# Two attention steps and two MLPs on one core: a prologue in another order, weights narrowed 512 wide at fixed steps, and the first MLP's product taken one step behind its halves

## The chip, the cores and the metric

The kernel runs on one core of one Trainium2 chip. A core has a matmul engine (PE, with its weight loads listed apart as PEld), a vector engine (DVE), an activation engine (ACT), a general engine (POOL), and SP, which here only issues DMAs. Each engine works through its own list of instructions in order, and waits on semaphores for what other engines make. The metric is the device time of one execution in microseconds (us). The kernel before takes 996.47 us, the median of three runs from 996.24 to 996.62.

## The reference

`x` is 12480 x 128, `inducing` 32 x 128; both MLPs have w_in 128 x 2048 and w_out 2048 x 128.

```python
def mab(q, kv):
    s = scale * (q @ kv.transpose(0, 2, 1))
    s = s - s.max(-1, keepdims=True)
    a = np.exp(s)
    a /= a.sum(-1, keepdims=True) + 1e-09
    return a @ kv
h = mab(I, x)                 # 32 x 128: the inducing rows attend to all of x
y = mab(x, h)                 # 12480 x 128: every row of x attends to h
y = (g * np.cos(g)) @ w_out   # first MLP, g = y @ w_in
y = (g * sigmoid(g)) @ w_out  # second MLP, g = y @ w_in
```

The weights arrive as 64-bit floats, which the chip does not compute with; the kernel reads them as pairs of 32-bit words and builds 32-bit floats itself.

## The kernel before

**Prologue.** `h` needs a pass over the whole of `x` before any row of the second attention can start. `x` is loaded in eight heads (L70) of 8, 16, 16, 16, 16, 16, 6 and 4 tiles of 128 rows. For each head, PE transposes its tiles (L389), ACT and DVE copy them out of PSUM (`untile`, L400 to L405), PE forms the scores (L420), DVE their maximum (`mx`, L430), ACT the exponentials (L480), DVE turns them (`et`, L503), and PE sums over `x` (L535). After the last head, `hT4` holds `h` transposed (L641), PE multiplies it into the first MLP's w_in (`project`, L657), and ACT and DVE make `hw` of it (L666, L669): the attention's second product and the first MLP's w_in are one matrix.

**Blocks and steps.** The 12480 rows are cut into 26 blocks of at most 512 rows. For each block a softmax over 32 weights per row gives `ahi` and `at`, the upper and lower half of the weights; four copies of them stacked on the partitions (`stk`, two buffers, used in turn) are the moving operand of the first MLP. The softmax is done by chunks of four blocks, the first chunk being two blocks. Blocks 0 and 1 get their stack from PE (L712) and an ACT copy (L720); all later ones from DMAs on SP's queue (`spread`, L296).

A block is eight units of 256 hidden columns, and step `s` of the main loop takes unit `s` through the first MLP and unit `s - 11` through the second: `mlp1_in(s)` (L768, PE) reads `stk` and `hw`; `mlp1_act(s)` (L797, ACT cosine; L801, DVE product; L808, DVE upper half `hi`); `mlp1_rest(s)` (L819, DVE lower half `lo`); `mlp1_out(s - D1)` with D1 = 2 (PE); `mlp2_in(s - 11)` (L877, PE), `mlp2_act` (L892 and L900 on ACT, L901 on POOL) and `mlp2_out(s - 13)` (PE). The hidden tile `h1` has two PSUM buffers, so `mlp1_in(s)` waits until DVE is done with unit `s - 2`; `h2` has one. A product into an output is either three passes over halves (`down`, L829) or, while the halves of the weights are not made yet, two full 32-bit matmuls (`down_whole`, L839): for the first two blocks of the first MLP (16 units), and the first block of the second (8 units).

**Narrowing.** Each of the four weight matrices is narrowed in 8 pieces of 256 columns: a DMA fetches 64-bit words into `raw`, ACT makes `body` and `tail` (L126, L127), DVE `sign` and the joined word (L132, L137), POOL adds the tail (L147). w_out and the second w_in are then split into halves by ACT (L161) and POOL (L162). 15 pieces are narrowed in the prologue, among the heads' work, and 17 in the main loop, from lists that the functions `words`, `signs`, `join` and `splits` take from. Every engine's order is the order in which the code is written.

Of the kernel before, what the change touches and what calls it, by code (L numbers as in the profile page):

```python
# [21 lines left out]
def tile_induced_attention_then_two_mlps(  # L22
# [47 lines left out]
    heads = [(90, 8), (0, 16), (16, 16), (32, 16), (48, 16), (64, 16), (80, 6), (86, 4)]  # L70
# [26 lines left out]
    EARLY = 15  # L97
    PC, RAW = 2 * P, 4
    cv = ctx.enter_context(tc.tile_pool(name="cv", bufs=2, reuse_waits="tile"))
# [3 lines left out]
        "out1": lambda j: w_out1.rearrange("(f p) d -> p f d", p=P)[:, 2 * j : 2 * j + 2, :],  # L103
        "out2": lambda j: w_out2.rearrange("(f p) d -> p f d", p=P)[:, 2 * j : 2 * j + 2, :],
    }
    raws = {}
    order = [(name, j) for name in ("in1", "out1", "in2", "out2") for j in range(NJ)]
    pieces = order[:EARLY]

    def fetch():  # L110
        if not pieces:
            return
        name, j = pieces.pop(0)
        raw = cv.tile([P, PC], I64, tag="raw", name="raw", bufs=RAW)
        dst = raw if name[0] == "i" else raw.rearrange("p (f d) -> p f d", f=2)
        nc.sync.dma_start(out=dst, in_=views[name](j))
        raws[name, j] = raw
# [3 lines left out]
    def narrow_words(name, j):  # L121
        words = raws.pop((name, j)).bitcast(I32).rearrange("p (n w) -> p n w", w=2)
        low, high = words[:, :, 0], words[:, :, 1]
        body = cv.tile([P, PC], F32, tag="body", name="body")
        tail = cv.tile([P, PC], I32, tag="tail", name="tail")
# [50 lines left out]

    def join(n=1):
        for _ in range(n):
            if not wait_join:
                signs()  # L180
            if wait_join:
                name, j = wait_join.pop(0)
                if name == "in1":
                    narrow_join(name, j, win[:, j * PC : (j + 1) * PC])
                elif name[0] == "o":
                    v = whole_of[name][:, 2 * j : 2 * j + 2, :].rearrange("p f d -> p (f d)")
                    narrow_join(name, j, v)
# [34 lines left out]

    def weigh_take(st):
        nt = st["span"][1]
        s2 = st["pool"].tile([P, nt, M], F32, tag="s2", name="s2t")
        nc.vector.transpose(s2.rearrange("p t m -> p (t m)"), st["ps"])  # L226
        st["e"] = s2

    def weigh_centre(st, eng):
        nt, s2 = st["span"][1], st["e"]  # L230
        m2 = st["pool"].tile([P, nt, 1], F32, tag="m2", name="m2")
        nc.vector.tensor_reduce(out=m2, in_=s2, axis=AX.X, op=ALU.max)
        eng.tensor_tensor(s2, s2, m2.to_broadcast([P, nt, M]), ALU.subtract)

    def weigh_exp(st):
        nc.scalar.activation(st["e"], st["e"], AF.Exp, scale=scale)  # L236

    def weigh_norm(st, eng, between=()):
        nt, e = st["span"][1], st["e"]
        sm = st["pool"].tile([P, nt, 1], F32, tag="sm", name="sm")  # L240
        between = iter(between)
        nc.vector.tensor_reduce(out=sm, in_=e, axis=AX.X, op=ALU.add)
        next(between, int)()
        nc.vector.tensor_scalar_add(sm, sm, 1e-9)
        next(between, int)()
        nc.vector.reciprocal(sm, sm)
        next(between, int)()
        eng.tensor_tensor(e, e, sm.to_broadcast([P, nt, M]), ALU.mult)

    def weigh_turn(st):  # L250
        at = st["pool"].tile([P, st["span"][1] * Q], F32, tag="at", name="at")
        nc.vector.transpose(at, st["e"].rearrange("p t m -> p (t m)"))
        st["at"] = at

    def weigh_split(st, eng):
        at = st["at"]
        n = st["span"][1] * Q
        hi = st["pool"].tile([P, n], F32R, tag="ahi", name="ahi")
        nc.scalar.copy(hi, at)
        eng.tensor_tensor(at, at, hi.bitcast(F32), ALU.subtract)  # L260
        st["hi"], st["lo"] = hi.bitcast(F32), at
# [12 lines left out]
    NU = NB * NJ  # L274
    stacks = {}
# [13 lines left out]
    def spread(b, st):  # L289
        t0 = chunks[blocks[b][0]][0]  # L290
        stack = stk[:, b % 2, :]
        for g, t, m, at, n in places(b):
            a = (t - t0) * Q
            for r in range(G):
                src = st["hi"] if r < 2 else st["lo"]
# [6 lines left out]
    with ExitStack() as pro:  # L302
# [31 lines left out]
        AHEAD = 2  # L334
        PRE = (2, 2)
        for k in range(AHEAD):
            load(k)
            for _ in range(PRE[k]):
# [711 lines left out]
```

## Time and profile before

| | us |
|---|---|
| median of 3 runs | 996.47 |
| profiled execution | 998.4 |
| its span (first to last instruction) | 996.6 |
| mean granted TensorE clock | 0.997 of full speed |

The page gives, for each engine, how long it was busy; rows of the trace give single instructions: start, duration, engine, line, output <- input, shape, and in brackets how long the engine stood idle before it and what it then waited for.

### The profile page before, as it was taken

The numbers are of one execution on the slowest core, as the hardware profiler recorded it, in microseconds if no ns is written. First come the engines' busy times: TensorE is split into PE (matmuls) and PEld (weight loads), VectorE is DVE, ScalarE is ACT, GpSimd is POOL, SyncE is SP. The second block draws the span as 40 slices with busy tenths as digits, with TensorE's granted clock in tenths as the row PEclk, the third lists the DMA queues.
The fourth block names the chain that finished last, engine by engine and source line by source line (L and its number), as shares of the span: only waits on it lengthen the run. The fifth ranks groups of instructions, "written<-read, shape, count | busy, mean of one in ns | idle before, by whom it ended". The sixth has DMA issues, their size and how long they took to land.

```text
span 996.6 us, 12618 instructions
## 1 busy us (share of the span) xinstructions
PE 970.7 (97%) x4687; PEld 775.5 (78%) x4687; DVE 782.6 (79%) x843; ACT 708.7 (71%) x810; POOL 512.7 (51%) x293
## 2 busy tenths in 40 slices
PE   9987999999999999999999999999999999999996
PEld 6644577788887788887788887788887788889996
DVE  4875588888888888888888888888888888767871
ACT  5778666777676777676777676777676777677774
POOL 2334355564555564555564555565555554565554
PEclk9999999999999999999999999999999999999999
DMA  8432010110110100110100100100100100000001
GB/s 284 134 108 62 22 21 1 22 25 9 22 19 3 22 13 9 22 19 4 22 12 11 22 16 5 22 12 11 22 16 6 21 11 8 18 18 16 9 8 17
DMA packets 65744, 27.98 MB, mean 28 GB/s; under 512 B 54312, under 2 KB 59656, under 8 KB 65672
## 3 DMA queue, kind: packets, MB, share of 16 engines
q1 hardware_dynamic: 65016, 26.98, 11.2%
q8 instruction: 39, 0.64, 0.3%
q14 instruction: 33, 0.27, 0.1%
q10 hardware_dynamic: 656, 0.09, 0.1%
HBM read 14.79 MB, written 6.39 MB: 21 GB/s over the span
## 4 chain that ended last, share of the span: by engine, by line
PE 88%; ACT 3%; issue 2%; DVE 2%; POOL 1%; POOLq 0%; DVEq 0%; ACTq 0%
PE acc L829 49%; PE h L877 27%; PE h L768 8%; PE acc L839 3%; ACT c L797 1%; ACT L892 1%; ACT s L892 1%; PE s L215 1%; DVE c L801 0%; DVE s2t L226 0%; ACT s2t L236 0%; PE hwps L657 0%; ACT L236 0%; DVE sign L137 0%; DVE sign L132 0%
## 5 line engine op out<-in xcount | busy, mean ns | idle before, releaser
L901 POOL TENSOR_TENSOR lo<-s,hi 128x1024 fp32r<-128x1024 f32 (+2 forms) x197 | 447.9, 2274 | 389.1 <-ACT hi L900 343.0
L829 PE MATMUL acc<-hi,wo 128*128 128x512 f32 (+2 forms) x1568 | 403.0, 379 | 0.0
L797 ACT ACTIVATE c<-h,half_pi 128x1024 f32<-128x1024 f32 (+2 forms) x208 | 221.1, 1063 | 158.0 <-PE h L768 157.9
L829 PEld LDWEIGHTS acc<-hi,wo 128*128 128x128 f32 x1568 | 285.5, 188 | 55.0 <-issue 1.4
L801 DVE TENSOR_TENSOR h<-h,c 128x1024 f32<-128x1024 f32 (+2 forms) x192 | 222.7, 1160 | 132.6 <-ACT c L797 132.3
L877 PE MATMUL h<-yhi,wi 128*128 128x512 f32 (+2 forms) x832 | 248.0, 380 | 6.7 <-ACT s L892 5.9
L892 ACT ACTIVATE s<-h 128x1024 f32<-128x1024 f32 (+2 forms) x208 | 202.3, 973 | 66.1 <-PE h L877 64.4
L829 PE MATMUL acc<-lo,wo 128*128 128x512 f32 (+2 forms) x784 | 232.8, 378 | 0.1
L808 DVE CAST hi<-h 128x1024 fp32r<-128x1024 f32 (+2 forms) x192 | 221.2, 1152 | 6.6
L819 DVE TENSOR_TENSOR lo<-h,hi 128x1024 fp32r<-128x1024 f32 (+2 forms) x192 | 220.2, 1147 | 5.7
L900 ACT CAST hi<-s 128x1024 fp32r<-128x1024 f32 (+2 forms) x197 | 196.6, 998 | 6.3
L877 PEld LDWEIGHTS h<-yhi,wi 128*128 128x128 f32 x832 | 151.3, 188 | 41.0 <-ACT s L892 10.4
L829 PEld LDWEIGHTS acc<-lo,wo 128*128 128x128 f32 x784 | 144.2, 188 | 29.2 <-POOL lo L906 0.4
L877 PE MATMUL h<-ylo,wi 128*128 128x512 f32 (+2 forms) x416 | 156.9, 377 | 0.0
L768 PE MATMUL h<-stk,hw 128*128 128x512 f32 (+2 forms) x416 | 128.8, 391 | 7.5 <-DVE c L801 6.8
L768 PEld LDWEIGHTS h<-stk,hw 128*128 128x128 f32 x416 | 76.1, 189 | 35.3 <-DVE c L801 12.2
L877 PEld LDWEIGHTS h<-ylo,wi 128*128 128x128 f32 x416 | 78.1, 188 | 14.5
L801 DVE TENSOR_TENSOR c<-h,c 128x1024 f32<-128x1024 f32 x16 | 19.5, 1222 | 19.8 <-ACT c L797 17.6
L839 PE MATMUL acc<-c,wf 128*128 128x512 f32 x64 | 31.2, 612 | 0.9 <-DVE ylo L863 0.9
L862 ACT CAST yhi<-acc 128x512 fp32r<-128x512 f32 (+2 forms) x26 | 14.6, 561 | 15.8 <-PE acc L829 12.3
L127 ACT ACTIVATE tail<-raw 128x256 int32<-128x256 uint32 x32 | 13.9, 435 | 13.6 <-POOL held L147 8.1
L863 DVE TENSOR_TENSOR ylo<-acc,yhi 128x512 fp32r<-128x512 f32 (+2 forms) x26 | 16.9, 651 | 8.4 <-ACT yhi L862 8.3
(138 smaller groups left out, 371.5 us busy)
## 6 DMA issues: line engine op xcount, KB each, us to landing
x_sb<-in_x_dram SPq DMA_DIRECT2D x10, 512.0 KB, 6.0
out_dram<-o SPq DMA_DIRECT2D x80, 64.0 KB, 2.0
raw<-in_moe_w_in_dram SPq DMA_DIRECT2D x16, 256.0 KB, 3.5
raw<-in_moe_w_out_dram SPq DMA_DIRECT2D x16, 256.0 KB, 2.8
stk<-ahi SPq DMA_DIRECT2D x40, 64.0 KB, 2.0
stk<-at SPq DMA_DIRECT2D x40, 64.0 KB, 2.0
x_sb<-in_x_dram SPq DMA_DIRECT2D x3, 192.0 KB, 4.5
out_dram<-o SPq DMA_DIRECT2D x34, 16.0 KB, 1.5
```

What stands on the lines that cost most here:

```text
L768: nc.tensor.matmul(ps[:, a, 0:n], lhsT=hw[f // 4][:, f % 4 * P : (f % 4 + 1) * P], rhs=stacks[b][:, 0:n], start=True, stop=True,)
L797: nc.scalar.activation(cs, h, AF.Sin, bias=half_pi, scale=1.0)
L801: nc.vector.tensor_tensor(cs if whole else h, h, cs, ALU.mult)
L808: nc.vector.tensor_copy(hi[:, :, 0:n], h)
L819: nc.vector.tensor_tensor(lo[:, :, 0:n], h, hi[:, :, 0:n].bitcast(F32), ALU.subtract)
L829: nc.tensor.matmul(acc[:, 0:n], lhsT=wt[:, 2 * j + a, :], rhs=gt[:, a, 0:n], start=(j == 0 and p == 0 and a == 0), stop=(j == NJ - 1 and p ...
L839: nc.tensor.matmul(acc[:, 0:n], lhsT=w[:, 2 * j + a, :], rhs=c[:, a, 0:n], start=(j == 0 and a == 0), stop=(j == NJ - 1 and a == 1),)
L863: nc.vector.tensor_tensor(lo[:, 0:n], y[:, 0:n], hi[:, 0:n].bitcast(F32), ALU.subtract)
L877: nc.tensor.matmul(ps[:, a, 0:n], lhsT=wt[:, fs], rhs=yt[:, 0:n], start=(p == 0), stop=(p == 2),)
L892: nc.scalar.activation(sv, hid2.pop(u)[:, :, 0:n], AF.Silu)
L900: nc.scalar.copy(hv, sv)
L901: nc.gpsimd.tensor_tensor(lv, sv, hv.bitcast(F32), ALU.subtract)
```

## The change

- **Prologue.** All of `x` is issued first, with three fetches of weights among its last heads; the heads are 8, 10, 16, 16, 16, 16, 11 and 5 tiles, and the ten tiles with the ragged end come second. Five pieces are narrowed there instead of fifteen, and they are 512 wide: one each beside heads 3 to 6, one after the last. DVE alone copies the last head's second half.
- **First blocks.** Before the main loop only block 0's softmax is finished, and only its stack comes from PE. Block 1's softmax is begun there (scores, centre, exponentials), normed at step 1, turned at 2, split at 3, and its stack is spread by DMA at step 4. Its weights lie in four groups of 128 columns, so the spread is 16 DMAs. The flag that picks the cosine's form is made after block 0's weights.
- **Main loop.** 11 pieces of 512 columns are narrowed at steps 0, 1, 2, 3, 5, 7, 9, 11, 12, 14 and 16 and split at fixed steps, with one buffer each of `body` and `sign`, two of `tail` and three of `raw`. Chunk 1's softmax takes steps 3 to 14 (its exponentials at 11 instead of 6), and block 2's stack is spread at step 15 instead of 13.
- **First MLP.** `mlp1_out` follows one step behind from unit 12 on, and full matmuls are used for 12 units instead of 16. `hi1` and `lo1` have two buffers instead of three.

```diff
-    heads = [(90, 8), (0, 16), (16, 16), (32, 16), (48, 16), (64, 16), (80, 6), (86, 4)]
+    heads = [(0, 8), (88, 10), (8, 16), (24, 16), (40, 16), (56, 16), (72, 11), (83, 5)]
...
-    EARLY = 15
-    PC, RAW = 2 * P, 4
-    cv = ctx.enter_context(tc.tile_pool(name="cv", bufs=2, reuse_waits="tile"))
+    EARLY = 5
+    PF = 4
+    PC, RAW = PF * P, 3
+    NP = NF // PF
+    raw = persist.tile([P, RAW, PC], I64, name="raw")
+    cv = ctx.enter_context(tc.tile_pool(name="cv", bufs=1, reuse_waits="tile"))
...
+    def narrow(name, j):
+
+        narrow_words(name, j)
+        yield
+        narrow_sign(name, j)
...
+            narrow_join(name, j, v)
...
+        fetch()
...
+    def begin(k):
+        step = narrow(*order[k])
+        next(step)
+        return lambda: next(step, None)
...
-        for k in range(AHEAD):
+        for k in range(NH):
             load(k)
-            for _ in range(PRE[k]):
+            if 3 <= k < 3 + RAW:
                 fetch()
...
+        beside = {3: 0, 4: 1, 5: 2, 6: 3}
         for i in range(end):
-            if i + AHEAD < NH:
-                load(i + AHEAD)
+            finish = None
...
             if i >= 1:
                 bias(i - 1)
                 exps(i - 1)
-                splits()
-                words()
+            if i in beside:
+                finish = begin(beside[i])
...
             if i >= 1:
                 turn(i - 1)
-            if 1 <= i < end - 1:
-                join()
+            if finish:
+                finish()
...
+        soft = [weigh_view(MT * b, MT, MT * b) for b in range(2)]
...
+        weigh_exp(soft[1])
         nc.scalar.activation(warm, ones, AF.Silu)
...
-    WHOLE1, WHOLE2 = 2, 1
+    WHOLE1, WHOLE2 = 12, 8
...
+    narrowing = dict(zip((0, 1, 2, 3, 5, 7, 9, 11, 12, 14, 16), order[EARLY:]))
+    splitting = dict(zip((4, 6, 8, 10), order[2 * NP : 3 * NP]))
+    splitting.update(zip((13, 15, 11, 12), order[NP : 2 * NP]))
+    splitting.update(zip((17, 18, 19, 20), order[3 * NP :]))
+
+    second = {1: "norm", 2: "turn", 3: "split"}
+    third = {3: "take", 5: "centre", 11: "exp", 12: "norm", 13: "turn", 14: "split"}
+    later = {0: "take", 2: "centre", 5: "exp", 7: "norm", 10: "turn", 11: "split"}
+
+    def d1(u):
+        return 2 if u < WHOLE1 else 1
...
         def fill(s):
-            for b in range(first_of[1], NB):
-                if s + (FILL0 if blocks[b][0] == 1 else FILL) == b * NJ:
-                    spread(b, ast)
+            for b in range(1, NB):
+                if s == (4 if b == 1 else b * NJ - (1 if b == 2 else FILL)):
+                    spread(b, chunk_soft[blocks[b][0]] if b > 1 else soft[1])
```

DVE in the loop over the heads, one turn from the scores' maximum to the next turn's copy: before,

```order
L430 TENSOR_REDUCE mx<-s_492 128x1
L503 STREAM_TRANSPOSE et<-e 128x512
L510 SCALAR_TENSOR_TENSOR zacc_167<-zacc_166,al,zk 128x1
L132 TENSOR_SCALAR sign<-raw 128x256
L137 SCALAR_TENSOR_TENSOR sign<-body,sign 128x256
L442 TENSOR_REDUCE rm<-misc 1x32
L402 COPY xT<-pt 128x2x256
```

and now, beside heads 3 to 6:

```order
L431 TENSOR_REDUCE mx<-s_414 128x1
L504 STREAM_TRANSPOSE et<-e 128x512
L511 SCALAR_TENSOR_TENSOR zacc_180<-zacc_179,al,zk 128x1
L143 TENSOR_SCALAR sign<-raw 128x512
L148 SCALAR_TENSOR_TENSOR sign<-body,sign 128x512
L443 TENSOR_REDUCE rm<-misc 1x32
L403 COPY xT<-pt 128x2x256
```

The two narrowing instructions stand at the same place and are twice as wide; the other pair of a turn, which stood behind `hacc`, is gone.

SP around the first stack that comes by DMA (`ahi` and `at` are the halves of the softmax's weights, `stk` the stack): before,

```order
L116 DMA raw<-in_moe_w_in_dram 128x256 x8
L116 DMA raw<-in_moe_w_out_dram 128x2x128 x8
L296 DMA stk<-ahi 32x512 x2
L296 DMA stk<-at 32x512 x2
```

where that is block 2's; and now, where block 1's comes first:

```order
L127 DMA raw<-in_moe_w_in_dram 128x512 x4
L297 DMA stk<-ahi 32x128 x2
L297 DMA stk<-at 32x128 x2
L297 DMA stk<-ahi 32x128 x2
L297 DMA stk<-at 32x128 x2
L297 DMA stk<-ahi 32x128 x2
L297 DMA stk<-at 32x128 x2
L297 DMA stk<-ahi 32x128 x2
L297 DMA stk<-at 32x128 x2
L127 DMA raw<-in_moe_w_out_dram 128x4x128 x4
L297 DMA stk<-ahi 32x512 x2
L297 DMA stk<-at 32x512 x2
```

Sixteen small DMAs are new, between the second w_in's last four fetches and the second w_out's.

POOL from step 2 on, in the changed kernel (line 158 is the narrowing's add, 173 the split's lower half, 261 the lower half `at` of a softmax's weights, 244 and 254 its centring and norming):

```order
L158 TENSOR_TENSOR wf_63<-sign,tail 128x512
L158 TENSOR_TENSOR tail<-sign,tail 128x512
L261 TENSOR_TENSOR at<-at,ahi 128x128
L173 TENSOR_TENSOR wi_1_768<-tail,wi_0_767 128x512
L158 TENSOR_TENSOR tail<-sign,tail 128x512
L244 TENSOR_TENSOR s_72<-s_72,m_73 128x512
L173 TENSOR_TENSOR wi_1_768<-tail,wi_0_767 128x512
```

Block 1's `at` stands behind the add of step 3's piece; before, block 1 had no `at` on POOL at all.

## Rows read from the trace of the kernel before

**Rows 1.** Stretches: us; PE, PEld, DVE, ACT, POOL busy; clock, DMA, GB/s.

```profile
54.09:94.67 40.58, 31.56 (x91) 15.72 (x91) 27.03 (x43) 32.00 (x55) 17.04 (x23) 0.96 0.28 83
...
140.00:945.00 805.00, 799.98 (x3612) 655.42 (x3611) 666.76 (x610) 581.47 (x582) 437.20 (x198) 1.00 0.08 15
```

**Rows 2.** PE's `mlp1_in`: start us, us, what, idle before. Units 0-1, 8, 9, 13.

```profile
54.09 1.20 PE L768 MATMUL h<-stk,hw 128*128 128x512 f32 x4 [0.67 <-ACT stk L720]
...
72.71 0.72 PE L768 MATMUL h<-stk,hw 128*128 128x512 f32 x2
79.16 1.22 PE L768 MATMUL h<-stk,hw 128*128 128x512 f32 x2 [4.00 <-DVE c L801]
...
94.67 1.03 PE L768 MATMUL h<-stk,hw 128*128 128x512 f32 x2
```

**Rows 3.** One turn of the loop over the heads, PE and DVE.

```profile
24.62 1.09 PE L389 MATMUL pt<-ident,x_sb 128*128 128x128 f32 x8
...
26.07 0.29 DVE L132 TENSOR_SCALAR sign<-raw 128x256 int32<-128x256 int32 x1
26.46 0.42 DVE L137 SCALAR_TENSOR_TENSOR sign<-body,sign 128x256 int32<-128x256 int32 x1
26.80 0.27 DVE L442 TENSOR_REDUCE rm<-misc 1x32 f32<-1x128 f32 x1
...
29.32 1.09 PE L389 MATMUL pt<-ident,x_sb 128*128 128x128 f32 x8
```

**Rows 4.** End of the prologue: `hT4`, ACT's copies of `hw` and `stk`.

```profile
45.22 0.28 DVE L641 COPY hT<-misc 128x128 f32<-128x128 f32 x1
...
50.10 2.03 ACT L666 CAST hw<-hwps 128x512 fp32r<-128x512 f32 x4
...
53.45 0.58 ACT L720 CAST stk<-st 128x512 fp32r<-128x512 f32 x1 [0.31 <-PE st L712]
```

**Rows 5.** Groups by form to 130 us: count, busy us, mean ns, idle before.

```profile
L797 ACT ACTIVATE c<-h,half_pi 128x1024 f32<-128x1024 f32 x20 | 22.2, 1112 | 3.9 <-PE h L768 3.9
L801 DVE TENSOR_TENSOR c<-h,c 128x1024 f32<-128x1024 f32 x16 | 19.5, 1222 | 19.8 <-ACT c L797 17.6 <-issue 2.1
...
L147 POOL TENSOR_TENSOR tail<-sign,tail 128x256 int32<-128x256 int32 x8 | 5.8, 724 | 11.6 <-DVE sign L137 8.0 <-ACT wi L161 2.5 <-ACT tail L127 1.1
...
L236 ACT ACT_TABLE_LOAD x1 | 1.3, 1283 | 0.0
...
L260 POOL TENSOR_TENSOR at<-at,ahi 128x512 f32<-128x512 f32 x1 | 1.3, 1280 | 0.0
L862 ACT CAST yhi<-acc 128x512 fp32r<-128x512 f32 x2 | 1.2, 588 | 3.2 <-PE acc L839 3.2
```

**Rows 6.** SP's issues: start us, us for all of them, count.

```profile
100.27 1.25 SPq L296 DMA_DIRECT2D stk<-ahi  x2
...
136.32 7.50 SPq L934 DMA_DIRECT2D out_dram<-o  x16
```

**Rows 7.** Page part 6: KB each, median us from issue to landing.

```profile
stk<-ahi SPq DMA_DIRECT2D x40, 64.0 KB, 2.0
...
out_dram<-o SPq DMA_DIRECT2D x34, 16.0 KB, 1.5
```

**Rows 8.** Granted clock (third from the right) after PE's pause from 75.16 us.

```profile
78.00:79.00 1.00, 0.00 (x0) 0.00 (x0) 1.00 (x1) 1.00 (x4) 0.00 (x0) 0.96 0.00 0
...
82.00:83.00 1.00, 1.00 (x4) 0.43 (x3) 0.93 (x4) 0.15 (x1) 0.72 (x1) 0.83 0.10 22
```

**Rows 9.** Chain of waits: one full product, and two products by halves.

```profile
93.51 1.72 PE acc L839 x4
...
138.33 2.78 PE acc L829 x12
```

**Rows 10.** A step in mid-run: DVE's last half, PE's next step.

```profile
516.63 1.22 DVE L819 TENSOR_TENSOR lo<-h,hi 128x1024 fp32r<-128x1024 f32 x1
516.90 0.62 PE L768 MATMUL h<-stk,hw 128*128 128x512 f32 x2
```

More of the change, by code (lines that the diff above doesn't have):

```diff
@@ L246, in weigh_norm @@
         nc.vector.reciprocal(sm, sm)
-        next(between, int)()
-        eng.tensor_tensor(e, e, sm.to_broadcast([P, nt, M]), ALU.mult)
+        eng.tensor_tensor(e, e, sm.to_broadcast(list(e.shape)), ALU.mult)
     def weigh_turn(st):
[L251 to L261, printed above, removed]
+        nc.vector.transpose(st["at"], flat(st["s2"]))
@@ L274, in tile_induced_attention_then_two_mlps @@
     NU = NB * NJ
+    chunk_soft = [weigh_view(*span) for span in chunks]
     stacks = {}
@@ new lines, in tile_induced_attention_then_two_mlps @@
+        top = ps_s.tile([P, W], F32, tag="s1", name="st")
+        for i, v in enumerate((hi0, lo0)):
+            for g, t, m, at, n in places(0):
+                nc.tensor.matmul(
+                    top[:, at : at + n],
+                    lhsT=pick[:, g, 2 - 2 * i : 6 - 2 * i, :].rearrange("p r m -> p (r m)"),
+                    rhs=v[:, t * Q : t * Q + n],
+                    start=(i == 0 and g == 0),
+                    stop=(i == 1 and g == G - 1),
+                )
+        nc.scalar.copy(stk[:, 0, :], top)
@@ new lines, in soften @@
+        def soften(st, what):
+            if what == "take":
+                ps = psh.tile([P, 2, 512], F32, tag="h2", name="s2")
+                weigh_scores(st, ps[:, 0, 0 : st["span"][1] * Q])
+                weigh_take(st)
+            elif what == "centre":
+                weigh_centre(st, nc.gpsimd)
+            elif what == "exp":
+                weigh_exp(st)
+            elif what == "norm":
+                weigh_norm(st, nc.gpsimd)
+            elif what == "turn":
+                weigh_turn(st)
+            elif what == "split":
+                weigh_split(st, nc.scalar.copy, nc.gpsimd)
@@ L973, in fill @@
+        def attend(s, early):
+            todo = [(soft[1], second.get(s)), (chunk_soft[1], third.get(s))]
+            for k in range(2, NK):
+                todo.append((chunk_soft[k], later.get(s + LEAD - first_of[k] * NJ)))
+            for st, what in todo:
+                if what and (what == "exp") == early:
+                    soften(st, what)
         def fill(s):
-            for b in range(first_of[1], NB):
-                if s + (FILL0 if blocks[b][0] == 1 else FILL) == b * NJ:
-                    spread(b, ast)
+            for b in range(1, NB):
+                if s == (4 if b == 1 else b * NJ - (1 if b == 2 else FILL)):
+                    spread(b, chunk_soft[blocks[b][0]] if b > 1 else soft[1])
```

291 lines of the change are left out of this document (108 added, 183 removed).

## Prediction, made before the changed kernel was run

> **What bounds the kernel now.** I read the busy times of each engine by stretches first. From 140 to 945 us PE is busy 799.98 of 805.00 us at a granted clock of 1.00 [rows 1]: whatever the change does there counts only if it adds or removes PE work, or makes PE wait. From 54.09 to 94.67, in the loop's first steps, PE is busy only 31.56 of 40.58, and no engine is busy all the time (ACT 32.00, DVE 27.03, POOL 17.04): a chain that passes from engine to engine sets the pace. Next I read PE's starts of `mlp1_in` one by one [rows 2]. Unit 0 starts at 54.09, unit 8 at 72.71, unit 9 after 4.00 us of waiting at 79.16, unit 13 at 94.67; from there on PE never waits long. So the kernel has three parts: a prologue of 54.09 us, a ragged stretch of 40.58 us, and a full PE. The change has to be priced in the first two, and by what it takes off PE's work in the third.
>
> **The prologue.** A turn of the loop over the heads takes 29.32 - 24.62 = 4.70 us [rows 3]. DVE's chain sets it, and `sign` and join stand in that chain, from 26.07 to 26.80, before `rm`: 0.73 us. The changed turn has the same two there, 512 wide. No row shows that form. A join of 256 is 0.42; doubling the columns adds some 0.27 (an ACT or DVE form of 512 is about 0.2 to 0.3 longer than one of 256), `sign` adds some 0.13: 0.4 us more a turn, bounds 0 and 0.73 (no change, twice as long). Turn by turn: the second head has six tiles less, about -2.0; the two following turns without narrowing -0.2 each; four turns with it +0.4 each; the last two heads have six tiles more, +1.8; narrowing that left the tail of the prologue -0.6. Sum +0.4, so `hT4` comes at about 45.7 instead of 45.22 [rows 4]. With the bounds it is between 42.5 and 47.
>
> From `hT4` to unit 0 it was 8.87 us. Now only block 0's softmax is on the way, at 128 columns instead of 256, and DVE has no narrowing there. But ACT is late next: its exponentials, the table load of 1.28, four copies into `hw` (2.03 for four) and one copy into `stk` (0.58) instead of two [rows 4, 5] end about 6.8 us after `hT4`. That is 2.05 less. The prologue's sum is -1.6, bounds -5 and +1.
>
> **Steps 0 to 12 without new waits.** Count t from unit 0. In steps 0 to 3 there is one buffer of `sign`: DVE's `sign` (start to join 0.52), join (0.70, and 0.14 until POOL starts), POOL's add, then the next `sign`. POOL's add of 256 takes 0.72 and its 512-wide subtraction 1.28 [rows 5]; I take 1.28 plus 0.04. That ring is 2.7 us a step, more than ACT's cosine and two narrowing instructions (2.1), and with a first `sign` at t = 3.3 and the softmax's small pieces the one of step 3 starts at 11.6. From step 4 on pieces come every second step and ACT has to copy the piece's upper half, made by POOL, before the next cosine: cosine 1.14, product 1.14 (1.11 and 1.22 busy), `sign` 0.52, join 0.84, add 1.32, copy 0.50 are 5.5 us for two steps. So the cosine of step 5 is at 14.8, that of step 11 at about 31.6. Then ACT has cosine, narrowing, a table load of 1.28, chunk 1's exponentials (0.53), another load, and the first SiLU: unit 1's `mlp2_in` can start at 37.8. PE has stood idle for some 5 us by then. A pause from 75.16 to 79.16 took the granted clock down (0.96 in the slice from 78, 0.83 in that from 82, half speed, the lower of its two levels, between) for 3.4 us [rows 8]; I take the same here, 1.6 us of PE work lost. PE then has no more pauses and reaches unit 2's `mlp2_in` at about t = 43.0. The mark of before is unit 13's start at t = 40.6, so this part costs +2.4. Bounds: -5 if no ring closes and ACT alone sets the pace, +4.
>
> **Block 1's stack.** Its lower half waits on POOL behind step 3's add, which ends at t = 14.2; it is done at 14.7. SP then issues its sixteen DMAs, two of them before. An issue of that line takes 0.58 to 0.62 (two take 1.25), sixteen small ones of another line 7.50, 0.47 each [rows 6]. By the first the last one is issued at 14.7 + 13 x 0.58 = 22.3 and lands 2.0 later (64 KB; 1.5 for 16 KB) [rows 7], at 24.3. Unit 8 could start at 20.05, when `h1` is free of unit 6, and ACT could take its cosine at 22.2. Now it is 25.4, 3.2 later, since PE paused for almost 5 us and comes back at half speed; the same slow matmuls hold up block 0's `yhi`, and with it the next cosine, by 1.25. That is +4.45: the new wait of this change. Bounds: 1.0 with 0.47 and 1.5, and 5.9 with 0.61 and a landing of 2.7. I take the values of the same line.
>
> The Trainium skill (DMA: Bandwidth & Descriptors, section "Anatomy of one DMA") puts a fixed cost of about 2.0 us on every DMA, whatever its size, and its section "Bandwidth" calls transfers under 64 KB descriptor-dominated, which speaks against sixteen of 16 KB. Landings of 1.5 at 16 KB and 2.0 at 64 KB agree in the main [rows 7]. By the page the last piece lands at 24.3 as above, by the 16 KB row 0.5 earlier, and the sum below would be 0.5 lower.
>
> **Block 2's stack.** Spread at step 15 for use at step 16. Its lower half stands on POOL behind step 14's add; four issues and a landing of 2.0 put it some 17 us after the mark above, and PE wants it after 16.1. PE is the bound by then, so what is late is lost: +1.1, bounds 0 and 2.5.
>
> **PE's work and the one-step product.** Four units of the first MLP go from a full product (1.72) to three passes (2.78 for two, 1.38 each) [rows 9]: -1.37. The two marks above differ by one `mlp1_in`, 0.46, which lies before the mark now: -0.46. The one-step product itself changes no work. It needs `lo` of unit s - 1 in step s; DVE's `lo` ends at 517.85, 1.2 us into the step whose `mlp1_in` starts at 516.90 [rows 10], and PE reads `hi` 3.0 and `lo` some 3.9 us into it. That is a slack of 2 us or more, and the largest extra that DVE has in one step (a transpose of 0.7 and the `ylo` of 0.7) leaves over half of it: nothing gained, nothing lost, as the drain still ends with the second MLP, eleven steps behind. Bounds 0 and +13 (0.5 in each of 26 blocks).
>
> **Sum.** -1.6 + 2.4 + 4.45 + 1.1 - 1.83 = +4.5. On the profiled execution (998.4, its span 996.6) that is 1002.9; it stands 1.9 above the median of the runs, so I put the difference on the median: 996.47 + 4.5 = **1001.0 us**.
>
> **Rivals.**
> - The stacks come in time. Then the two stack terms are gone and the sum is -1.0, 995.4. For it: small DMAs were issued at 0.47 and landed in 1.5 us, and POOL could reach block 1's half earlier if steps 0 to 3 are shorter. Against it: sixteen issues take 7.5 us at the best rate in the trace, which is as long as three of these steps.
> - Faster, on the other side: the rings do not close. DVE's join and POOL's add run beside ACT's work, steps 0 to 10 go at the pace of ACT's cosine, narrowing and copies (1.9 a step) or PE's two products (2.2). The cosine of step 11 then comes at 25.5 instead of 31.6, the stack is asked for earlier but also split earlier, and waits about 1.5: -1.6 - 3.6 + 1.5 - 1.8 = -5.5, 991.0. It decides as soon as POOL's 512-wide add ends before DVE's next `sign` is due. For it: POOL was busy 17.04 of 40.58 us. Against it: DVE and ACT waited for each other and for POOL in those very steps while no engine was full [rows 1].
> - The one-step product makes PE wait for `lo` in the steps with DVE's extra work: +13, about 1009. Against it: the slack of 2 us.
> - It doesn't do what it says: `hT4` comes no earlier although x is first, since the loop over the heads waits for DVE and PE and not for x. That is in the sum already.
>
> **Chances.** The forecast with its waits 0.56; the stacks in time 0.22; the rings open 0.17; `lo` late 0.05. A difference under 0.2% (2 us) is about what a measurement of this kernel cannot tell from none. The forecast's own range is 998.0 to 1005: nearly all of it is slower, a little the same. The stacks in time is the same for the greater part, sometimes faster. So faster 0.21, same 0.22, slower 0.57. For 8 in 10 the range must take in the stacks in time and the lower bounds of the rings: 992.5 to 1004.5.
>
> **What would show it.** In the profile after: `hT4` between 44.5 and 47 and unit 0 about 6.8 us behind it; `sign` of steps 0 to 3 about 2.7 us apart; PE idle before unit 8 by 3 to 5 us, released by a DMA into `stk`, with the granted clock at 0.5 behind it; a second pause of about 5 us at step 12 behind two table loads; 1 us before unit 16, again a DMA; no wait of PE for `lo`. If unit 8 starts without a pause the stack terms are wrong; if unit 13 starts before 93 us, the early steps are; if PE waits once a block, the one-step product is.

## The result, and the profile after

The changed kernel takes 1007.22 us (median of four runs, 1005.34 to 1008.78) against 996.55 for the kernel before: 1.0100 times as long, 95% interval 1.0071 to 1.0128. That is 10.7 us slower, where +4.5 was forecast and 1004.5 was the upper end of the range. The profiled execution is the shortest of the four, 1005.34 with a span of 1003.5. In the experiments below, three executions of 1371 to 5469 us, far beyond the others of their kernels, are left out (one of `e10_exp0`, two of the kernel before).

First the stretches, as in [rows 1]; the first one goes from unit 0 to unit 13, as 54.09 to 94.67 did.

```profile
49.99:100.78 50.79, 36.87 (x91) 18.50 (x91) 31.16 (x42) 33.03 (x44) 19.65 (x17) 0.83 0.34 99
140.00:945.00 805.00, 798.50 (x3581) 652.05 (x3580) 664.22 (x606) 580.23 (x575) 434.88 (x195) 1.00 0.08 15
```

In the full part PE is busy 1.5 us less; the last row below shows where it waits instead. The ragged part was 40.58 us and is 50.79, at a mean granted clock of 0.83 instead of 0.96. PE's rows show where, as in [rows 2]: start, duration, what, and in brackets the idle time before and what ended it (line 752 is `mlp1_in`, 859 `mlp2_in`).

```profile
49.99 0.74 PE L752 MATMUL h<-stk,hw 128*128 128x512 f32 x2 [1.42 <-ACT stk L698]
...
53.96 1.22 PE L752 MATMUL h<-stk,hw 128*128 128x512 f32 x2 [1.89 <-DVE c L784]
...
68.71 0.72 PE L752 MATMUL h<-stk,hw 128*128 128x512 f32 x2
...
76.43 1.19 PE L752 MATMUL h<-stk,hw 128*128 128x512 f32 x2 [5.28 <-DMA stk<-at]
...
96.56 1.22 PE L859 MATMUL h<-yhi,wi 128*128 128x512 f32 x2 [5.13 <-ACT s L874]
...
100.78 1.02 PE L752 MATMUL h<-stk,hw 128*128 128x512 f32 x2
101.64 0.63 PE L859 MATMUL h<-yhi,wi 128*128 128x512 f32 x2
...
119.04 0.70 PE L752 MATMUL h<-stk,hw 128*128 128x512 f32 x2 [1.11 <-DMA stk<-at]
...
164.56 0.72 PE L859 MATMUL h<-yhi,wi 128*128 128x512 f32 x2 [0.42 <-DVE s L239]
```

Unit 0 starts at 49.99, 4.10 earlier than in [rows 2]. Before unit 8, PE waits 5.28 us for a DMA into `stk`, and before unit 1's `mlp2_in` 5.13 us for the first SiLU. Unit 13 starts at t = 50.79, where t counts from unit 0 (before: 40.58). The last row is a wait that was 0.18 before; it comes five times, once in each later chunk (2.20 us in all, 0.72 before).

SP's issues of block 1's stack, as in [rows 6], and the time from issue to landing, as in [rows 7]:

```profile
63.98 1.25 SPq L297 DMA_DIRECT2D stk<-ahi  x2
66.17 1.14 SPq L297 DMA_DIRECT2D stk<-at  x2
...
73.69 1.22 SPq L297 DMA_DIRECT2D stk<-at  x2
...
stk<-at SPq DMA_DIRECT2D x8, 16.0 KB, 1.8
```

Sixteen issues of about 0.61 us; the last one starts at 74.3 and PE goes on at 76.43, 2.1 later. A landing takes 1.8 us, between the 1.5 of stores of the same size and the 2.0 of 64 KB in [rows 7]. The Trainium skill (DMA: Bandwidth & Descriptors, section "Anatomy of one DMA — SWDGE (gpsimd) path") gives a fixed cost of some 2.0 us, for DMAs that GpSimd issues; the prediction left that condition out. These are issued by SP, and their 1.8 is near it. The granted clock (third from the right), as in [rows 8]:

```profile
52.00:54.00 2.00, 0.11 (x2) 0.04 (x1) 1.62 (x3) 2.00 (x4) 1.28 (x1) 0.50 0.53 101
...
76.00:78.00 2.00, 1.57 (x3) 1.16 (x4) 0.00 (x0) 0.34 (x1) 0.65 (x1) 0.50 0.72 188
...
82.00:84.00 2.00, 2.00 (x5) 0.77 (x5) 0.00 (x0) 0.00 (x0) 0.00 (x0) 0.86 0.00 0
...
98.00:100.00 2.00, 2.00 (x6) 1.43 (x5) 1.90 (x2) 1.64 (x4) 0.38 (x1) 0.59 0.00 0
```

It is at its lower level three times: from 51.8 to 58.7, from 75.7 to 82.6 and from 96.2 to 99.6 (slices of 0.5 us). At the stack's pause that lasted 6.8 us, twice what [rows 8] showed (3.4), and at the pause of step 12 3.4.

### The profile page after: what moved, and what is told of

Same layout as the page of the kernel before. It is cut to its first block, busy times and chain, and to the rows that moved or that the text cites. A ratio compares the mean times of both kernels' runs of the same rounds, so it can differ in the third digit from the quotient of the medians.

```text
span 1003.5 us, 12438 instructions
## 1 busy us (share of the span) xinstructions
PE 968.4 (96%) x4667; PEld 774.1 (77%) x4667; DVE 788.3 (79%) x824; ACT 703.3 (70%) x766; POOL 509.0 (51%) x268
## 4 chain that ended last, share of the span: by engine, by line
PE 87%; DVE 5%; ACT 4%; issue 2%; SPq 1%; POOL 1%; DMA 0%; DVEq 0%; ACTq 0%; POOLq 0%
PE acc L811 48%; PE h L859 26%; PE h L752 8%; PE acc L821 2%; ACT c L781 2%; PE s L421 1%; SPq L297 1%; ACT L874 1%; ACT s L874 1%; DVE sign L148 1%; DVE h L784 1%; PE pt L388 1%; DVE hi L790 1%; DVE lo L801 1%; DMA stk<-at 0%
## 5 line engine op out<-in xcount | busy, mean ns | idle before, releaser
L811 PE MATMUL acc<-hi,wo 128*128 128x512 f32 (+2 forms) x1584 | 409.3, 380 | 0.0
L784 DVE TENSOR_TENSOR h<-h,c 128x1024 f32<-128x1024 f32 (+2 forms) x196 | 227.5, 1161 | 140.9 <-ACT c L781 140.6
L811 PEld LDWEIGHTS acc<-hi,wo 128*128 128x128 f32 x1584 | 288.5, 188 | 57.8 <-issue 2.2
L811 PE MATMUL acc<-lo,wo 128*128 128x512 f32 (+2 forms) x792 | 235.4, 378 | 0.1
L790 DVE CAST hi<-h 128x1024 fp32r<-128x1024 f32 (+2 forms) x196 | 226.1, 1153 | 6.8
L801 DVE TENSOR_TENSOR lo<-h,hi 128x1024 fp32r<-128x1024 f32 (+2 forms) x196 | 225.1, 1148 | 5.9
L821 PE MATMUL acc<-c,wf 128*128 128x512 f32 x48 | 26.7, 685 | 0.9 <-DVE ylo L845 0.9
L906 DVE STREAM_TRANSPOSE o<-acc 128x512 f32<-128x512 f32 (+2 forms) x26 | 17.5, 673 | 7.6 <-PE acc L811 7.6
L784 DVE TENSOR_TENSOR c<-h,c 128x1024 f32<-128x1024 f32 x12 | 14.6, 1213 | 9.0 <-ACT c L781 9.0
```

The lines of the kernel that those rows point to most:

```text
L784: nc.vector.tensor_tensor(cs if whole else h, h, cs, ALU.mult)
L790: nc.vector.tensor_copy(hi[:, :, 0:n], h)
L801: nc.vector.tensor_tensor(lo[:, :, 0:n], h, hi[:, :, 0:n].bitcast(F32), ALU.subtract)
L811: nc.tensor.matmul(acc[:, 0:n], lhsT=wt[:, 2 * j + a, :], rhs=gt[:, a, 0:n], start=(j == 0 and p == 0 and a == 0), stop=(j == NJ - 1 and p ...
L821: nc.tensor.matmul(acc[:, 0:n], lhsT=w[:, 2 * j + a, :], rhs=c[:, a, 0:n], start=(j == 0 and a == 0), stop=(j == NJ - 1 and a == 1),)
L906: nc.vector.transpose(o.rearrange("p t d -> p (t d)")[:, 0:n], acc2.pop(b)[:, 0:n])
```

## The experiments

All were timed beside the kernel before, in three groups (its medians there: 997.78 for e0, e1, e2, e4; 998.16 for e3, e5, e6, e7; 997.20 for e8 to e11). "A" and "B" are the theories of the expectation; t counts from unit 0 of the same run.

| run | edit, in short | us | ratio to before, interval |
|---|---|---|---|
| e0_after | none | 1007.64 | 1.0097, 1.0081 to 1.0112 |
| e1_stack_pe | block 1's stack by PE, wo2 moved | 1008.74 | 1.0116, 1.0100 to 1.0131 |
| e2_warm | zeros on PE in steps 0, 1, 11 | 1013.49 | 1.0162, 1.0142 to 1.0181 |
| e4_both | e1 and e2 | 1015.89 | 1.0177, 1.0163 to 1.0192 |
| e3_before_d1 | before, one-step product alone | 1001.23 | 1.0033, 1.0020 to 1.0045 |
| e5_stack_wo1 | block 1's stack by PE, wo2 in place | 1002.35 | 1.0047, 1.0034 to 1.0060 |
| e6_tail_warm | zeros back in the last head | 1006.91 | 1.0088, 1.0075 to 1.0101 |
| e7_all | e5, e6, last pieces later | 1021.59 | 1.0229, 1.0215 to 1.0242 |
| e8_sign2 | e5, second `sign` buffer | 1001.19 | 1.0040, 1.0025 to 1.0054 |
| e10_exp0 | e5, chunk 1's exponentials in the prologue | 994.60 | 0.9989, 0.9976 to 1.0002 |
| e11_spins | e5, zeros on PE in step 12 | 1000.67 | 1.0032, 1.0020 to 1.0044 |
| e9_best | e5, e6, e8, e10 | 994.49 | 0.9970, 0.9961 to 0.9979 |

**e0_after.** No edit.

> The changed kernel once more, for a second profile and for times beside the edits. In the first profile PE waited 5.28 us before unit 8 for the last DMA into stk, 5.13 us at step 12, and 1.89 us before unit 2, and the granted clock fell to 0.50 behind each of these. Theory A (each pause lets the clock fall, and how long it stays down differs from run to run): 1005 to 1009 again, the longer runs with the lower mean clock. Theory B (the pauses themselves differ, for instance because the DMAs land at other times): the mean clock is the same in short and long runs.

1005.62 to 1008.05, and the shortest run has the highest mean clock (0.991; the two longest 0.988), as A says, with four runs. The pauses are the same: the wait for `stk` is 5.28 to the digit. The clock differs: at step 12's pause (5.16) it is down for 6.8 us instead of 3.4, and from unit 12 to unit 13 it takes 11.54 us instead of 10.38. Another 1.25 us has no such cause: the first eight transposes of the prologue take 1.97 us instead of 1.09 at a granted clock of 1.00 in both profiles, and unit 0 starts at 51.25.

**e1_stack_pe and e5_stack_wo1: block 1's stack without DMAs.** The sixteen DMAs go; `pick`, which must outlive the prologue, needs a place.

```diff
+        def stack_by_pe():          # in step 6
+            top = psh.tile([P, 2, 512], F32, tag="h2", name="st")[:, 0, :]
+            for i, v in enumerate((soft[1]["hi"], lo_b1)):
+                for g, t, m, at, n in places(1):
+                    nc.tensor.matmul(top[:, at : at + n], lhsT=pick[...], rhs=v[...], ...)
+            nc.scalar.copy(stk[:, 1, :], top)
...
-                if s == (4 if b == 1 else b * NJ - (1 if b == 2 else FILL)):
+                if b > 1 and s == b * NJ - (1 if b == 2 else FILL):
```

> Block 1's stack is built by eight matmuls on PE in step 6 and one ACT copy, as block 0's is, instead of sixteen DMAs; the rest is the changed kernel. Theory A (the sixteen issues, 0.6 us each, are what unit 8 waits for): unit 8 starts 21.5 us after unit 0 instead of 26.4, no half clock behind it, and the whole comes down by 5 to 8 us, to 999 to 1002. Theory B (the chains over ACT, DVE and POOL would hold unit 8 and its followers back all the same): unit 8 is earlier, unit 11 is not, and the time falls by less than 2 us, to 1005 or more.

> Block 1's stack by PE as in the run e1_stack_pe, but pick and the lower halves lie in wo1's second tile, which is free until step 11, and wo2 stays where the changed kernel has it. There unit 13 was 6.6 us earlier, and all of it was lost again at 4.63 us a step instead of 4.593. Theory A (that step came from where wo2's tile was put): 4.593 a step again, 1000 to 1002. Theory B (the step comes from the stack built on PE, or from the earlier start): 4.63 again, 1007 or more.

PE in e1, units 0 and 8, and unit 2's `mlp2_in`:

```profile
50.11 0.74 PE L762 MATMUL h<-stk,hw 128*128 128x512 f32 x2 [1.41 <-ACT stk L707]
...
71.78 0.71 PE L762 MATMUL h<-stk,hw 128*128 128x512 f32 x2
...
95.00 0.62 PE L869 MATMUL h<-yhi,wi 128*128 128x512 f32 x2
```

Unit 8 starts at t = 21.67 without a wait and unit 13 is 6.6 us earlier than in the profile after, as A says; yet the time did not fall at all. PE lost it again in the full part. Its groups from 300 to 800 us in e1 (mean ns behind the comma):

```profile
L821 PE MATMUL acc<-hi,wo 128*128 128x512 f32 x845 | 231.9, 396 | 0.0
...
L762 PE MATMUL h<-stk,hw 128*128 128x512 f32 x210 | 65.8, 394 | 0.0
```

and in e5, where `pick` and the lower halves lie in a part of `wo1` that is free until step 11, and `wo2` has its old place:

```profile
L820 PE MATMUL acc<-hi,wo 128*128 128x512 f32 x852 | 231.1, 393 | 0.0
...
L761 PE MATMUL h<-stk,hw 128*128 128x512 f32 x212 | 65.9, 391 | 0.0
```

The same matmuls at a granted clock of 1.00 are 3 ns longer in e1, and a step takes 4.64 us ((237.35 - 204.86) / 7) instead of 4.593. e4, which moves the same tile, has 396 and 394 too; e0 and e2, timed beside e1 without that move, have 393 and 391. e5 is 5.3 us faster than the changed kernel: A, and what e1 lost again it lost by the tile's place. What in the placement does it is open; e1 moved much else by the size of that tile. PE in e5:

```profile
72.91 0.70 PE L761 MATMUL h<-stk,hw 128*128 128x512 f32 x2
...
84.82 1.03 PE L761 MATMUL h<-stk,hw 128*128 128x512 f32 x2
91.00 1.22 PE L868 MATMUL h<-yhi,wi 128*128 128x512 f32 x2 [5.15 <-ACT s L883]
...
96.09 1.03 PE L761 MATMUL h<-stk,hw 128*128 128x512 f32 x2
96.95 0.62 PE L868 MATMUL h<-yhi,wi 128*128 128x512 f32 x2
```

No wait before unit 8 (72.91). Unit 2's `mlp2_in` is at t = 96.95 - 51.25 = 45.70, in e1 at 95.00 - 50.11 = 44.89, in the profile after at 51.65. The two differ by the clock: at step 12's pause it was down for 6.8 us in e5, for 3.4 in e1 and in the profile after. So like for like the stack by DMA, with the clock behind it, cost 51.65 - 44.89 = 6.8 us. The pause at step 12 stays.

**e2_warm and e4_both: the clock in the first steps.**

```diff
         nc.scalar.copy(stk[:, 0, :], top)
+        keep_warm(spin, 4)
...
+            if s in IDLE:           # {1: 5, 11: 13}
+                spin = psh.tile([P, 2, 512], F32, tag="h2", name="spin")[:, 0, 0:P]
+                for _ in range(IDLE[s]):
+                    nc.tensor.matmul(spin, lhsT=idle, rhs=idle, start=True, stop=True)
```

> Matmuls on a tile of zeros are put where PE stands idle in the changed kernel: 4 behind block 0's stack, 5 in step 1, 13 in step 11 (0.3 us each at full clock). The sixteen DMAs stay. Theory A (the half clock from 52 to 58.5 us costs 1.5 us at unit 4, that from 96 to 99.3 about 1.5 more): the clock stays at 1.00 there and the time falls by 2 to 4 us, to 1003 to 1005. Theory B (in these steps ACT, DVE and POOL set the pace, PE has time to spare at either clock): within 1 us of the changed kernel, 1006 or more.

> Both edits together: block 1's stack on PE, and the matmuls on zeros. Theory A: 997 to 1000, about the sum of the two, with a narrow spread of the runs. Theory B (chains over the other engines): 1004 or more.

Both are slower, by a fault of the edit. PE in e2:

```profile
97.07 5.87 PE L976 MATMUL spin<-idle 128*128 128x128 f32 x26 [7.34 <-ACT s L876]
```

The matmuls on zeros in step 11 took the PSUM tile of `mlp2_in` and so waited for the first SiLU, and unit 1's `mlp2_in` behind them. The first steps are still to be read. From 50 to 60 us the clock is 1.00 in e2 and 0.83 in e0, unit 0 starts at 51.24 and 51.25, and unit 5 at 64.26 and 64.27: there a full clock gained nothing. That is B for steps 0 to 5; for step 11 this run says nothing.

e4 shows something else, in the prologue, whose instructions up to there are those of the changed kernel:

```profile
38.00:40.00 2.00, 1.62 (x31) 1.04 (x24) 1.20 (x5) 0.89 (x4) 0.31 (x1) 0.65 0.66 229
40.00:42.00 2.00, 2.00 (x25) 1.71 (x27) 0.82 (x4) 2.00 (x6) 0.00 (x0) 0.50 0.01 4
```

The clock falls while PE idles between the last heads, stays down until 49, and unit 0 starts at 54.45.

**e6_tail_warm.** The change had also taken three short runs of matmuls on zeros out of the last head, which its description above does not name. These are the first two.

```diff
         transposes(end, 1)
+        keep_warm(gather(end - 2), 2)
         untile(end, 1)
         row_max(end - 1)
+        keep_warm(gather(end - 2), 2)
```

> The changed kernel with the two short runs of matmuls on zeros put back that the change had taken out of the last head (behind its second transposes and behind the row maximum). In the run e4_both, whose prologue is the changed one, the clock fell to 0.50 at 38.7 us and unit 0 came at 54.45 instead of 50 to 51.3. Theory A (this happens in about half of the changed kernel's executions, and it is why they lie 3 us apart): the median falls by 1 to 3 us, to 1004.5 to 1006.5, and the spread to 2 us. Theory B (a rare event, and the spread comes from later pauses): 1007 to 1008 as before.

0.7 us faster, 1005.78 to 1007.51, inside the intervals of both: by itself it decides nothing. Over all profiles there is a pattern. Without these matmuls unit 0 started at 49.99, 51.25, 50.11, 51.24, 51.25 and, with a clock that had fallen between 38 and 41 us, at 52.61, 54.45 and 54.53 (e8, e4, e11; e10's prologue is another); with them at 51.02, 51.05 and 51.41 (e6, e7, e9), and the clock did not fall there. And e10, without them, has six runs from 994.14 to 994.60 and five from 996.41 to 998.73; e9, with them, ten from 993.98 to 994.77 and one at 996.44. That points to a cost of 1 to 4 us in some executions. It is not shown: three falls in eight profiles against none in three can be chance, and e9 differs from e10 by the second `sign` buffer too.

**e3_before_d1.** The kernel before with one line changed.

```diff
-            v = s - D1
-            if 0 <= v < NU:
+            for v in range(max(s - 2, 0), min(s, NU)):
+                if v + (2 if v < WHOLE1 * NJ else 1) == s:
```

> The kernel before, with one part of the change alone: the first MLP's product one step behind its halves, from unit 16 on (the first with halves there). Theory A (lo is ready over 2 us before PE reads it, the product costs nothing): within 1 us of the kernel before, PE waits for no lo. Theory B (it is this part that makes the changed kernel slower, a little in each of 26 blocks): 3 to 10 us slower. Its profile also gives a second look at the old prologue, where unit 0 started at 54.09.

3.1 us slower, at the lower end of B. The waits of PE in the full part that the kernel before has not, or shorter, are of two sorts, of which these are the first rows (line 829 is the first MLP's product, 877 `mlp2_in`):

```profile
123.06 1.19 PE L829 MATMUL acc<-hi,wo 128*128 128x512 f32 x4 [1.66 <-DVE ylo L863]
...
160.08 0.73 PE L877 MATMUL h<-yhi,wi 128*128 128x512 f32 x2 [0.42 <-DVE s2t L226]
```

The first is the step where the delay goes from two to one, and comes once. The second comes in each chunk's scoring step: DVE's transpose of the scores holds up `mlp2_in`, which takes over their PSUM tile; 2.20 us in five chunks against 0.72 in the kernel before (0.18 four times). Together they are the 3.1. DVE around that transpose, in the kernel before and in e3:

```profile
155.95 0.72 DVE L226 STREAM_TRANSPOSE s2t<-s 128x512 f32<-128x512 f32 x1 [0.26 <-PE s L215]
...
161.79 0.69 DVE L863 TENSOR_TENSOR ylo<-acc,yhi 128x512 fp32r<-128x512 f32 x1 [0.32 <-ACT yhi L862]
...
158.72 0.68 DVE L863 TENSOR_TENSOR ylo<-acc,yhi 128x512 fp32r<-128x512 f32 x1
159.32 0.70 DVE L226 STREAM_TRANSPOSE s2t<-s 128x512 f32<-128x512 f32 x1
```

Before, DVE stands ready for the scores, and the finished block's `ylo` comes a step later. With a delay of one, that `ylo` falls into the scoring step and stands ahead of the transpose. The same five waits of 2.20 are in the changed kernel. `lo` itself is never waited for.

**e7_all.** e5 and e6 together with

```diff
-    narrowing = dict(zip((0, 1, 2, 3, 5, 7, 9, 11, 12, 14, 16), order[EARLY:]))
+    narrowing = dict(zip((0, 1, 2, 3, 5, 7, 9, 13, 15, 17, 18), order[EARLY:]))
```

> Block 1's stack by PE with wo2 in its place, the matmuls on zeros in the last head, and the narrowing of the last four pieces moved from steps 11, 12, 14, 16 to 13, 15, 17, 18. Theory A: -6.8 for the stack, -2 for the clock in the prologue, -1 to -2 for a shorter pause at step 12 (1.2 us of ACT's work leave step 11): 996 to 998.5, no slower than the kernel before. Theory B (the pause at step 12 takes over what the others give back): 1000 to 1003.

Worse than either theory. The pause at step 12 fell from 5.15 to 4.05, but the second MLP's full products need those pieces from step 13 on:

```profile
102.45 3.45 PE L832 MATMUL acc<-s,held 128*128 128x512 f32 x4 [4.93 <-POOL held L162]
```

Three such waits, 4.9 us each: those steps of the table had no slack, so e7 says nothing on the sum of its other two parts.

**e8_sign2.**

```diff
+        if EARLY <= k < 12 and k % 2:
+            sign = spare_sign()     # the store's tile, free in these steps
+        else:
             sign = cv.tile([P, PC], I32, tag="sign", name="sign")
```

> The run e5_stack_wo1 (block 1's stack on PE, 1002.35) with a second buffer for sign in steps 0 to 4, in a tile that is free there, so that nothing else moves. Theory A (DVE's sign waits for POOL's add of the piece before, and this ring paces steps 0 to 3): unit 5 starts 11 us after unit 0 instead of 13.0, unit 12 1.5 to 2 us earlier than its 33.6, and the time falls to 1000 to 1001. Theory B (ACT and DVE together set the pace, the ring is slack): less than 0.5 us, 1002 to 1003.

The gap between the second and third `sign` falls from 2.67 us to 2.27, where `sign` had waited 0.32 us for POOL's add; of that 0.34 us are left at unit 12 (t = 33.23, e5 33.57). Unit 5 starts later (13.64, e5 13.00), at a clock that stayed down longer in this profile, but that does not reach unit 12. So B holds for the steps: the ring closes, and is worth 0.3 us. The 1.2 us in the medians have overlapping intervals.

**e10_exp0, e11_spins, e9_best: the pause at step 12.** e10 takes the exponentials, and with them two table loads, out of step 11:

```diff
+        weigh_scores(chunk_soft[1], ps)          # prologue, ahead of project(3)
...
+        weigh_take(chunk_soft[1])
+        weigh_centre(chunk_soft[1], nc.gpsimd)   # behind lo0
...
         nc.scalar.copy(stk[:, 0, :], top)
+        weigh_exp(chunk_soft[1])
+        nc.scalar.activation(warm, ones, AF.Silu)
...
-    third = {3: "take", 5: "centre", 11: "exp", 12: "norm", 13: "turn", 14: "split"}
+    third = {5: "norm", 7: "turn", 9: "split"}
...
-                if b > 1 and s == b * NJ - (1 if b == 2 else FILL):
+                if b > 1 and s == b * NJ - (6 if b == 2 else FILL):
```

> The run e5_stack_wo1 with chunk 1's scores and exponentials moved from steps 3 to 11 into the prologue, ahead of the table load that is there anyway, so that step 11 has no exponentials and no two table loads (3.2 us of ACT); its turn and split move to steps 7 and 9, block 2's stack is spread at step 10. Theory A (the pause of 5.15 us before unit 1's second MLP is those 3.2 us): the pause falls to about 2 us, unit 0 comes 0.5 us later, no DMA is waited for at unit 16: 997.5 to 1000. Theory B (the first SiLU would be late for another reason, DVE or PE): 1001.5 or more.

> The run e5_stack_wo1 with 14 matmuls on zeros in step 12, between unit 12's first product and the pause of 5.15 us, into a PSUM bank that is still free. Theory A (the half clock behind this pause, 91 to 95 us, delays all that follows, since PE is the bound from there on): the clock stays at 1.00 and the time falls by 1.5 to 2.5 us, to 1000 to 1001. Theory B (as in steps 0 to 5, where a full clock gained nothing): 1002 to 1003.

> Together: block 1's stack on PE, the second sign buffer, chunk 1's exponentials in the prologue with block 2's stack spread at step 10, and the matmuls on zeros put back in the last head. Theory A: the sum of the parts, 994 to 998, at or below the kernel before. Theory B (one wait hands over to the next): 1000 or more.

ACT at step 11 in the changed kernel:

```profile
92.25 1.28 ACT L247 ACT_TABLE_LOAD   x1
93.55 0.63 ACT L247 ACTIVATE s<-s 128x512 f32<-128x512 f32 x1
94.19 1.28 ACT L874 ACT_TABLE_LOAD   x1
95.49 1.02 ACT L874 ACTIVATE s<-h 128x1024 f32<-128x1024 f32 x1
```

and PE in e10:

```profile
85.37 1.03 PE L773 MATMUL h<-stk,hw 128*128 128x512 f32 x2
88.21 0.73 PE L880 MATMUL h<-yhi,wi 128*128 128x512 f32 x2 [1.80 <-ACT s L895]
```

The 3.2 us between 92.25 and 95.49 are gone, the pause is 1.80 instead of 5.15, the clock stays at 1.00 behind it, and from unit 12 to unit 13 it takes 5.65 us instead of 11.27. No DMA is waited for at unit 16. e10 is 6.7 us faster than e5 on the mean of the runs (996.04 against 1002.70), 7.8 by medians, more than A gave. Some 1.2 us of it are not the edit's: its three new tiles moved others, and eight steps of the full part take 36.69 us (200.09 to 236.78) instead of 36.74 (201.70 to 238.44), an estimate over 195 steps.

e11 fills the pause (14 calls are 28 matmuls here; the idle time behind them is what is left of it; the first and last rows are units 12 and 13):

```profile
88.10 1.02 PE L763 MATMUL h<-stk,hw 128*128 128x512 f32 x2
88.97 3.29 PE L995 MATMUL spin<-wo 128*128 128x128 f32 x28
94.32 0.73 PE L870 MATMUL h<-yhi,wi 128*128 128x512 f32 x2 [2.07 <-ACT s L885]
...
97.13 1.04 PE L763 MATMUL h<-stk,hw 128*128 128x512 f32 x2
```

Its clock is 1.00 from 84 to 100 us, where e5 is at 0.50 from 89.0 to 95.8. From unit 12 to unit 13 it takes 9.03 us. Behind the same pause it takes 10.38, 10.46 and 10.53 where the clock was down for 3.4 us (the profile after, e1, e8), and 11.27, 11.54 and 11.54 where it was down for 6.8 (e5, e0, e6). So here the clock costs 1.4 or 2.4 us: PE is the bound from there on. The median is 1.7 lower than e5's, as A says, but the intervals overlap, and it is only 0.5 below e8's.

e9 is the version that beats both kernels: 994.49, 0.30% below the kernel before (0.21 to 0.39) and 13 us below the changed one. Its eight steps take 36.69 us as in e10, the kernel before's 36.74, so that about 1.2 of these 3 us come from where its tiles lie.

## Why the prediction was wrong

The direction and the places were right: each of the pauses stands where it was forecast, before unit 8 for a DMA, at step 12 behind two table loads, and 1.1 us before unit 16. Two terms of the ragged part were too small, and that is the step that failed. Its terms, with what the traces give:

| term | forecast | measured |
|---|---|---|
| prologue | -1.6 | -4.1 in the profile after, -2.2 on the mean of the eight profiles without the matmuls of e6 |
| steps 0 to 12 without new waits | +2.4 | +4.3 (e1: 44.89 - 40.58) |
| block 1's stack | +4.45 | +6.8 (51.65 - 44.89) |
| block 2's stack | +1.1 | +1.1 |
| PE's work, one-step product | -1.83 | -1.2 (span behind the mark 901.86 instead of 901.93, without the 1.1) |

With -4.1 that is +6.9, the difference of the two spans. e1 gives the second and third lines because the clock was down for 3.4 us at its step 12, as forecast and as in the profile after; by e5, where it was 6.8, they are +5.1 and +5.95. The medians are 10.7 apart, since the profiled execution of before lay 1.9 above its median and that of after 1.9 below. e0's profiled execution, at its median, is 9.2 above the span of before: -2.8 in the prologue, +11.5 up to unit 2's `mlp2_in` (t = 52.05), +0.6 behind it. That the total was not missed by more is luck: the profile after gained 2.5 us in the prologue that were not forecast.

**Block 1's stack** is the larger miss, by 2.3 us, and most of it is the price of the half clock. ACT's copy of block 0's `yhi`, in the profile after and in e1:

```profile
84.04 0.58 ACT L844 CAST yhi<-acc 128x512 fp32r<-128x512 f32 x1 [4.76 <-PE acc L821]
...
77.35 0.58 ACT L854 CAST yhi<-acc 128x512 fp32r<-128x512 f32 x1
```

Unit 8's cosine comes at t = 27.7 instead of 23.9, 3.8 later, where 3.2 was forecast: the issues took 0.61 instead of 0.58, and the last DMA was used 2.1 us after its issue instead of 2.0. The slow matmuls behind it were to cost another 1.25 at `yhi` and the next cosine; that cosine is 6.8 later (34.5 instead of 27.7), so they cost 3.1. The clock was down for 6.8 us there, and 3.4 had been taken from one pause of the kernel before.

**Steps 0 to 12** are too short by 1.9 us. The pace of 2.7 us was met at first (`sign` at 51.15, 53.82, 56.49), but the third gap is 3.92, and the cosine of step 5 comes at t = 16.3 (e1, e5 and the profile after; forecast 14.8). One row of DVE in the changed kernel explains up to 0.95 of these 1.5; the same instruction stands first as it runs in the prologue:

```profile
45.34 0.28 DVE L252 TENSOR_SCALAR sm<-sm 128x4 f32<-128x4 f32 x1
...
57.94 1.23 DVE L252 TENSOR_SCALAR sm<-sm 128x4 f32<-128x4 f32 x1
59.21 0.18 DVE L253 RECIPROCAL sm<-sm 128x4 f32<-128x4 f32 x1
59.30 1.19 DVE L784 TENSOR_TENSOR c<-h,c 128x1024 f32<-128x1024 f32 x1
```

and POOL beside it:

```profile
57.85 1.29 POOL L158 TENSOR_TENSOR wf<-sign,tail 128x512 int32<-128x512 int32 x1 [1.40 <-DVE sign L148]
```

An instruction on four columns lasts 1.23 us and ends with POOL's add, 59.17 against 59.14; e5 and e8 show the same. It lies on the chain of waits that ended last. The Trainium skill (SBUF — State Buffer, section "SBUF: two separate sides") says that DVE and POOL share one port pair as an exclusive lock: a DVE instruction in a two-port mode, or with two SBUF inputs against a POOL instruction that reads SBUF, and a POOL instruction do not run side by side, and whichever starts first holds the pair for its whole length. The row agrees, POOL having started 0.09 us earlier; that this DVE form uses both ports is not shown here. The wider narrowing brings adds of 1.29 instead of 0.72, and block 1's norm stands among them at step 1. Without POOL beside it was not tried, so its full share stays argued, and the rest of the 1.5 is open. The ring through the one `sign` buffer, the explanation given for the pace, closes at one step and is worth 0.3 us (e8). ACT's next `body` waits for DVE's join as well (0.35 and 0.43 us). From step 5 to 11 the forecast of 5.5 us for two steps holds nearly (16.93 for six steps). How long the clock stays down at step 12, 3.4 us or 6.8, differs between executions of the same program (the profile after and e0) and decides another 1 us.

**The one-step product** costs something, where nothing was forecast. The slack of `lo` was read rightly, and the rival on `lo` is refuted. But the wait was looked for at `lo` alone: the `ylo` that was counted there as extra work of DVE falls into the scoring step, ahead of the transpose that `mlp2_in` waits for (e3). That is +1.5 in the changed kernel, and 3.1 as a part by itself. The term measured is lower than -1.83 + 1.5, by 0.8 us that lie behind the last matmul: it ends 6.2 us before the end of the profile, in the kernel before 7.0 and in e5 7.9, which is chance.

**The prologue** gained more than forecast. `hT4` came at 42.68, where 45.7 was forecast, and 44.5 to 47 as a sign. The turns with a 512-wide narrowing take 5.10 us, 0.4 more, as forecast; the miss is in the first two heads: the third starts at 10.57 instead of 15.38, 4.8 us earlier, and 2.0 were forecast for the smaller second head. Of this, 1.25 was not there in e0, e2 and e5, and the runs of matmuls on zeros that left the last head, which the sum has at nothing, may take more: in three of eight profiles the clock fell there. From `hT4` to unit 0 it is 7.3 us, near the 6.8.

The rival with the stacks in time fell with the 5.28 us; the one with open rings fell with the cosine of step 11, at t = 33.2 in e1 and e5, where it wanted 25.5.

## What to carry to other kernels

When a transfer's use is set by the calendar, count its issues: sixteen at 0.61 us on one queue were 9.7 us, and eight small matmuls did the same between two products at no visible cost (unit 7's cosine at t = 21.8 with either). Price a pause of PE by what runs behind it: at half clock it cost nothing where other engines set the pace, 1.4 or 2.4 us where PE did, and 3.1 where the next chain waited for PE's slow matmuls. When a delay between stages is shortened, look at every instruction that moves into another step with it, not at the moved operand alone. Keep tiles in their places when an edit is to be timed, and compare profiles whose clock fell for the same time.

## What the runs showed of the hardware

- The place of tiles in SBUF changed PE's pace: with `wo2`'s second tile moved, matmuls of 512 columns went from 391 and 393 ns to 394 and 396 at full clock (e1 and e4 against e0, e2 and e5), 4.593 to 4.64 us a step, some 6.4 us in all by the medians of e1 and e5. In e10 and e9 other moves made eight steps 0.05 us shorter.
- A DVE instruction on 128x4 lasted 1.23 us beside POOL's add, 0.28 without it, in the profiles of the changed kernel, e5 and e8.
- At a pause of 5.1 to 5.3 us the clock fell to half and stayed there for 3.4 us in some executions and for 6.8 in others, of the same program and at the same place (step 12: the profile after and e0). At 38 to 41 us some profiles lost it where others, with the same instructions up to there, did not.
